# A fused long-convolution and Mish-MLP block on one core: the 660 operations in another total order

## The chip, the cores and the metric

The kernel runs on one core of one Trainium2 chip. The metric is the device time of one execution in microseconds; runs are compared by their medians. The engines are called as in the profile: PE is the matmul array (PEld its weight loads), DVE the vector engine, ACT the scalar engine, POOL the GpSimd engine, SP the sync engine, which here only issues DMAs.

## The reference

All tensors are bf16, the sequence S is 2048, the model width D 640, the inner width F 1728.

```python
h  = x + q_ln * y                       # q_ln = layernorm(x), x = A_q
# kv: 4-tap causal shift convolution of k, times v
kv = (sum over t of k[s-t] * shift_k[:, t]) * v
# y: causal convolution along the sequence with a filter as long as it (FFT of length 2S), plus a skip
y  = irfft(rfft(kv, 2S) * rfft(ssm_k, 2S))[:S] + kv * ssm_D
# the MLP: act(u) = u * tanh(softplus(u)) (Mish)
out = h + act(layernorm(h) @ w1 + b1) @ w2
```

## The kernel before, in words

The convolution is done by matmuls with the tables of a two-stage transform of 128 x 16 points. The channels are held in five chunks of 128 (dc = 0 to 4). The program first builds a list of 660 named operations; each has its engine (or a choice), its dependencies and an emit function (`OP`, class `_Op`). A string `ORDER` then names all 660 in one total order, and `_ordered` emits them in it. An engine works through its own operations strictly in the order of that list, whatever else is ready; between engines only the dependencies count. A token may carry two marks: `@n` places the operation's result in PSUM slot n (there are four slots of 128 x 1024 f32, and a slot is filled again only when its last reader is done), and `:a`, `:d`, `:p` choose ACT, DVE or POOL where the first choice is not meant. DMAs named `d_..`, `sw..` and `tr..` are issued by SP in the order of the list; `d_cst`, `d_sk` and `d_dr` are issued by ACT, and the three small loads of the bias by POOL, within `small`.

The operations by name, in the order of the data:

- `wm` (L292): nine matmuls of zeros that warm PE up; `warm` (L284): loads ACT's function table.
- `d_n0..4`: the filter's five chunks; `dadd0..4` (L370) adds the skip ssm_D to the first tap, with `dsel`, `dcol` (L279, L280) made from `d_dr`; `k1pe0..4` (L376): 16 transposes each, `k1ev` empties them to SBUF.
- `s1kpe dc_g` (L396, L397): the filter's first transform stage, 20 PSUM tiles, emptied by `s1kev`; it needs `d_cst`. `s2kpe_f`, `s2kev_f` (L422): its second stage, in 22 blocks of up to six frequencies, with the table G (`d_g0..7`).
- `b1pe` (L498): transposes the MLP's bias b1, which `small` has loaded (L298, L300); `c_b1` copies it out. `cfpe` (L304): spreads the shift taps (`d_cst`, `d_sk`) over the partitions; `coef` (L309) copies them out, `wsh0..3` (L317) build the shift matrices from them.
- `ktpe`, `ktev` (L341): transposes of k; `kspe dc_h` (L357, L358): the shift convolution, 10 tiles; `kv dc_h` (L362): times v, on DVE.
- `s1vpe`, `s1vev`: the first transform stage of V, the product kv (20 tiles); `s2v0`, `s2v2`, `s2v1`: its second stage, 20 blocks.
- `sw dc_i` (L450): ten DMAs that swap the halves of the filter's spectrum; they need every `s2kev`. `pr dc_f` (L461): 20 products of the two spectra on DVE.
- `i1pe`, `i1ev` (L479): the inverse's first stage, 20 tiles, each needing all four products of its chunk; `i2a`, `i2b`, `i2pe` (L531): its second stage, one per tile of 128 tokens; `y` empties it.
- `ln1_t`, `ln1p t`, `lnx t` (L510 to L524): layernorm of x for token tile t, on DVE, POOL, and ACT or POOL; `wb`, `h` (L538, L540): times y, plus x; `bn`, `pow`, `hc` (L544 to L559): the second layernorm; `trpe`, `trev` (tiles 0 and 1 on PE) or `tr` (a DMA transpose, the others): its result with the channels on partitions.
- `m1pe u_f`, `hb u_f` (L598 to L620): the MLP's first matmul with Mish, in five units of 256, 256, 512, 512 and 512 tokens; `m2pe t` (L663, L671), `res`, `d_out`: its second, the sum with h and the store. `d_w1..` and `d_w2a..c` load the weights.

The casts from PSUM to SBUF of most stages (`ev`, L261 on ACT, L263 on DVE) share one line; they are told apart by their tiles: uv for k's transposes, V and the inverse, ks for the filter and y.

Of the kernel before, what the change touches and what calls it, by code (L numbers as in the profile page):

```python
# [30 lines left out]
ktpe0_3 ktpe0_2 s1kev1_2 ktpe2_0@3 ktpe2_3 ktpe2_2 d_v2 ktpe2_1 ktpe0_1 ktev2 ktpe1_0@1 ktev0:a ktpe1_1 ktpe1_3 ktpe1_2 s1kpe3_3@0 d_g5 ktev1 ktsh2
s1kpe4_0@3 s1kev3_3 s1kpe1_1@2 ktsh0 s1kev4_0:d d_v3 s1kpe4_2@1 wsh0 s1kev1_1 s1kpe3_0@0 s1kev4_2:d s1kpe2_3@3 s1kev3_0 d_g3 ktpe4_0@2 ktpe4_2 ktpe4_3
s1kev2_3 ktsh1 ktpe3_0@1 ktpe4_1 ktpe3_3 ktev4 ktpe3_1 ktpe3_2 s2kpe_6@0 s2kpe_12@3 ktev3 s2kev_6 kspe0_0@2 s2kev_12 s2kpe_18@0 kv0_0 ktsh3 kspe2_0@1
s2kev_18 ktsh4 s2kpe_42@3 kv2_0 kspe3_0@2 s2kev_42 s2kpe_96@0 kv3_0 s2kpe_24@1 s2kev_96 kspe4_0@3 s2kev_24 kspe1_0@2 kv4_0 s2kpe_108@0 kspe1_1@1 kv1_0
# [8 lines left out]
s2v2pe_80@2 pr1_96 s2v2ev_32 s2v2pe_112@1 s2v2pe_64@3 s2v2ev_112 pr1_0 s2v2pe_48@0 s2v2ev_64 s2v2pe_0@1 pr0_96 s2v2ev_0 s2v2pe_16@3 pr1_32 s2v2ev_16
s2v1pe_96@1 pr0_64 s2v2ev_48 i1pe1_1@3 s2v2ev_80 s2v2pe_96@0 pr3_0 s2v1ev_96 i1pe1_2@2 pr3_32 i1ev1_1 s2v1pe_64@1 pr0_32 s2v2ev_96 s2v1pe_0@3 i1ev1_2
pr0_0 s2v1pe_32@0 s2v1ev_0 pr3_64 i1pe1_3@2 d_w14 s2v1ev_64 d_w10 i1pe0_2@3 pr3_96 d_w11 s2v1ev_32 d_w12 i1pe0_1@1 pr4_0 d_w13 i1ev1_3 d_t2m i1pe3_3@0
i1ev0_1 pr2_96 i1pe3_1@2 i1ev3_3 pr2_64 i1pe3_0@1 i1ev0_2 i1pe0_3@0 pr2_0 i1ev3_0 i1pe0_0@3 pr2_32 i1ev3_1 i1pe3_2@1 i1ev0_3 pr4_96 i1pe2_0@2 i1ev0_0
# [687 lines left out]
```

## Time and profile before

| | |
|---|---|
| three runs | 225.21, 226.12 (median), 226.17 us |
| profiled execution: span of its instructions | 223.5 us; its own full time is not on the page |
| busy: PE, PE weight loads | 214.0, 157.6 us |
| busy: DVE, ACT, POOL | 133.2, 133.0, 58.9 us |
| moved by DMA | 30.98 MB, mean 139 GB/s |

The span runs from the first to the last instruction. A matmul is pipelined, so a busy PE need not be at its peak. A row of the timeline reads: start, length, engine, line, operation, output and input tiles, shape, count, and in brackets the idle time before it with what ended it. A row of the groups reads: line, engine, operation, tiles, shape, count, then busy time, mean ns of one, and idle time before.

### The profile page before, as it was taken

What the parts mean: (1) busy time and instruction counts of PE and PEld (TensorE: products, weight loads), DVE (VectorE), ACT (ScalarE), POOL (GpSimd) and SP (SyncE); (2) the same over time, 40 slices, a digit from 0 to 9 for tenths busy, and PEclk for the clock granted to TensorE, in tenths of its full rate; (3) what the DMA queues carried; (4) which work ended last, traced back from release to release, by engine and by line L of the source; (5) the groups of instructions that cost most, each with busy time, mean ns of one, the idle gap of its engine ahead of it and who ended that gap; (6) DMA issues with size and microseconds to landing.
All of it is one profiled execution on the core that took longest, in us unless ns stands there. A gap on an engine that the chain in (4) does not pass through costs nothing.

```text
span 223.5 us, 6119 instructions
## 1 busy us (share of the span) xinstructions
PE 214.0 (96%) x2645; PEld 157.6 (70%) x2650; DVE 133.2 (60%) x232; ACT 133.0 (59%) x182; POOL 58.9 (26%) x120
## 2 busy tenths in 40 slices
PE   7899999999879999889999999999999999999994
PEld 2899999888869999458877644444567444766763
DVE  2776899999989999889878999100002200022122
ACT  2389888999999999999983015565600075200000
POOL 5147620102860005347887523100000000000000
PEclk9999999999999999999999999999999999999999
DMA  5999994372991789303004443500001100010211
GB/s 181 390 413 409 412 374 121 143 239 93 375 415 69 258 331 290 124 0 62 1 0 62 84 123 91 118 0 0 3 0 59 59 3 0 0 56 6 76 54 49
DMA packets 19563, 30.98 MB, mean 139 GB/s; under 512 B 10704, under 2 KB 14928, under 8 KB 18768
## 3 DMA queue, kind: packets, MB, share of 16 engines
q1 hardware_dynamic: 19104, 30.46, 39.0%
q8 instruction: 21, 0.34, 0.7%
q10 hardware_dynamic: 336, 0.12, 0.2%
q14 instruction: 6, 0.05, 0.1%
q0 software_dynamic: 96, 0.00, 0.0%
HBM read 20.42 MB, written 2.62 MB: 103 GB/s over the span
## 4 chain that ended last, share of the span: by engine, by line
PE 70%; DVE 13%; DMA 9%; ACT 4%; issue 2%; SPq 1%; POOL 1%; DVEq 0%
PE ps L663 26%; PE ps L598 25%; DVE ks L461 6%; DMA ks<-in_B_w_dram 4%; DMA ks<-ks 3%; PE ps L396 3%; PE ps L422 3%; ACT uv L261 3%; DMA ks<-in_A_ssm_k_dram 3%; PE ps L341 2%; PE ps L376 2%; DVE ks L263 2%; PE ps L357 2%; DVE ra L362 1%; PE ps L397 1%
## 5 line engine op out<-in xcount | busy, mean ns | idle before, releaser
L620 ACT ACTIVATE ks<-ps,b1s 128x512 bf16<-128x512 f32 (+1 forms) x69 | 36.1, 610 | 42.8 <-PE ps L598 30.3
L663 PE MATMUL ps<-ks 128*128 128x320 bf16 (+2 forms) x420 | 58.4, 299 | 0.0
L598 PE MATMUL ps<-G 128*128 128x512 bf16 (+1 forms) x320 | 57.0, 336 | 0.3
L688 DVE TENSOR_TENSOR rb<-ps,rb 128x640 bf16<-128x640 f32 x15 | 11.7, 816 | 68.9 <-PE ps L671 66.5
L663 PEld LDWEIGHTS <-ks 128*128 128x128 bf16 x420 | 40.6, 98 | 17.2 <-issue 1.3
L598 PEld LDWEIGHTS <-G 128*128 128x128 bf16 x325 | 31.3, 98 | 24.4 <-issue 1.1
L261 ACT CAST uv<-ps 128x1024 bf16<-128x1024 f32 x49 | 45.2, 1197 | 0.0
L261 ACT CAST ks<-ps 128x960 bf16<-128x960 f32 (+3 forms) x49 | 39.8, 905 | 8.1 <-PE ps L397 5.0
L461 DVE TENSOR_TENSOR ks<-ks,uv 128x2048 bf16<-128x2048 bf16 x20 | 23.1, 1225 | 0.7 <-DMA ks<-ks 0.7
L422 PEld LDWEIGHTS <-G 128*128 128x128 bf16 x512 | 20.9, 96 | 3.1 <-issue 2.5
L479 PE MATMUL ps<-a_t,ks 128*128 128x128 bf16 x320 | 18.8, 219 | 0.4 <-DVE ks L461 0.3
L479 PEld LDWEIGHTS <-ks 128*128 128x128 bf16 x320 | 18.3, 113 | 0.7 <-DVE ks L461 0.6
L422 PE MATMUL ps<-uv,G 128*128 128x64 bf16 (+1 forms) x384 | 12.8, 186 | 1.8 <-ACT uv L261 1.8
L544 DVE BATCH_NORM_STATS2 st<-rb 128x6 f32<-128x320 bf16 x32 | 14.0, 478 | 0.1
L515 POOL TENSOR_SCALAR ve<-mv 128x1 f32<-128x1 f32 x16 | 4.7, 292 | 34.9 <-DVE mv L511 34.2
L510 DVE BATCH_NORM_STATS2 st<-rb 128x6 f32<-128x320 bf16 x32 | 13.7, 471 | 0.0
L263 DVE CAST uv<-ps 128x1024 bf16<-128x1024 f32 x11 | 12.9, 1204 | 0.1
L362 DVE TENSOR_TENSOR ra<-ps,rb 128x1024 bf16<-128x1024 f32 x10 | 11.9, 1222 | 0.7 <-PE ps L358 0.5
L524 POOL TENSOR_SCALAR ra<-rb,r,nmr 128x640 bf16<-128x640 bf16 x8 | 8.9, 1118 | 10.0 <-PE ps L397 9.3
L422 PE MATMUL ps<-ks,G 128*128 128x160 bf16 x128 | 11.2, 230 | 0.0
L396 PE MATMUL ps<-cst,ra 128*64 128x128 bf16 x160 | 10.6, 219 | 0.7 <-ACT uv L261 0.5
L263 DVE CAST ks<-ps 128x1024 bf16<-128x1024 f32 (+1 forms) x9 | 10.5, 1197 | 0.5 <-PE ps L422 0.3
(71 smaller groups left out, 256.1 us busy)
## 6 DMA issues: line engine op xcount, KB each, us to landing
ks<-ks SPq DMA_DIRECT2D x10, 512.0 KB, 6.2
G<-tab_g SPq DMA_DIRECT2D x8, 512.0 KB, 11.4
...
```

The source lines that it names most:

```text
L261: nc.scalar.copy(o, i)
L263: nc.vector.tensor_copy(o, i)
L362: nc.vector.tensor_tensor(kv_w[:, m, :, 8 * h:8 * h + 8, :], p_.f32().rearrange("p (l t d) -> p d t l", l=4, t=8), raw_v[:, 8 * h:8 * h + ...
L396: nc.tensor.matmul(ps[0:64, dgl, :], lhs, mc, start=True, stop=True)
L422: nc.tensor.matmul(p_.f32()[:, o:o + n], g_v[:, f, :], src[:, :, f, :], start=True, stop=True)
L461: nc.vector.tensor_tensor(o, o, v, ALU.mult)
L479: nc.tensor.matmul(pz[:, dgl, :], KS[:, k, b, :, l], a12[:, k, :], start=k == 0, stop=k == 1)
L510: nc.vector.bn_stats(st1[:, t, hh, :], xt(t)[:, hh * 320:(hh + 1) * 320])
L544: nc.vector.bn_stats(st2[:, t, hh, :], xt(t)[:, hh * 320:(hh + 1) * 320])
L598: nc.tensor.matmul(ph[:, o:o + w], w1[:, dc, fc * P:fc * P + P], lt[:, dc, 0:w], start=dc == 0, stop=dc == NDC - 1)
L620: nc.scalar.activation(hb[:, fc, 0:n], p_.f32()[:, i * 512:i * 512 + n], ACT.Mish, bias=b1s[:, fc:fc + 1], scale=1.0)
L663: nc.tensor.matmul(p_.f32()[:, o:o + n], lhs, w2[:, k, cols:cols + n], start=fc == 0, stop=single and fc == 13)
```

## The change

Only the string `ORDER` changes: the same 660 names in another total order, with other PSUM slots and, for some, another engine. On ACT's side, `k1ev4`, `ktev0`, `y0`, `y13`, `trev0` and some casts go to DVE and others come from it (`ktev3`, for one); `wsh2` and `wsh3` go from POOL to DVE; `lnx4`, `lnx8`, `lnx9` and `lnx11` go from ACT to POOL and `lnx13` the other way. The first lines of both lists, the stretch in which the filter's second stage meets V's first, and the stretch from the inverse to the MLP:

```diff
 ORDER = """
-d_dr wz idn d_n0 cz wm@0 small lane d_n1 d_cst d_sk d_n2 warm d_n3 d_n4 d_g0 dsel dcol dadd0 d_k2 k1pe0@1 d_k3 dadd1:p k1pe1@2 d_a12 k1ev0b d_k0 k1ev0
-s1kpe0_3@3 k1ev1 s1kpe0_1@0 s1kev0_3 d_k1 s1kpe0_0@1 dadd2 s1kev0_1 s1kpe1_3@2 s1kev0_0:d dadd3:p d_g4 s1kpe0_2@3 k1pe2@0 s1kev0_2 dadd4:p d_g1
-s1kev1_3 kz b1pe@1 k1pe4@3 k1ev2 c_b1 cfpe@2 k1pe3@1 k1ev4:a coef d_v0 s1kpe2_0@0 k1ev3 wsh1 s1kpe2_1@2 s1kev2_0 s1kpe4_3@3 d_g7 s1kev2_1:d s1kpe3_1@1
...
-s2kev_54 s2kpe_60@3 s2kev_84 ln1_0 kspe2_1@1 s2kev_60 s2kpe_48@0 kv2_1 ln1p0 s1vpe0_2@2 s2kev_48 s1vpe1_1@3 s1vev0_2:d s1vpe2_1@1 d_x2 s1vev1_1
...
-s1vpe0_3@1 s1vev1_2 s1vpe1_3@0 s1vev0_3:d s1vpe0_1@2 s1vev1_3 s1vpe3_0@3 s1vev0_1:d s1vpe4_1@1 s1vev3_0 s2kpe_30@0 s1vev4_1:d s2v0pe_0@2 s2kev_30
...
-pr4_32 i1pe1_0@0 i1ev2_0 i1pe2_2@3 pr4_64 i1ev1_0 i1pe2_1@2 ln1_8 i1ev3_2 i1pe2_3@0 i1ev2_2 ln1_6 ln1p8 i1pe4_3@1 i1ev2_3 ln1_11 i1pe4_0@3 ln1p6
...
-trpe1@2 y11 i2pe7@3 hc0 y13 h2 trpe0@1 trev1:a wb3 i2pe6@0 bn2 trev0:a i2pe10@2 y7 m1pe0_3@1 h3 lnx11 pow2 bn3 m1pe0_2@3 y6 hc2 y10 pow3 ln1_7
...
+idn wz small d_n0 warm d_sk lane d_dr d_cst wm@0 cz dsel dcol dadd0 b1pe@1 d_n1 cfpe@2 coef d_n2 d_n3 k1pe0@3 dadd2:p c_b1 d_n4 dadd1 k1pe1@0 k1ev0
+k1ev0b s1kpe0_1@1 k1ev1 dadd3 s1kpe0_0@2 wsh1 d_g0 dadd4:p wsh2:d k1pe2@3 d_k2 s1kev0_1 k1pe3@0 s1kev0_0 d_k3 k1ev2 wsh0 s1kpe1_3@1 k1ev3 s1kev1_3
...
+ktpe4_0@3 ktpe4_3 ktpe4_1 ktpe4_2 kspe1_1@0 s2kpe_120@1 ktev4 s2kpe_0@2 s2kev_120 d_v1 kspe1_0@3 s2kpe_114@1 s2kev_0 kv1_1 ktsh4 ktsh0 kspe3_0@0
...
+s2kpe_66@1 kspe0_1@3 s1vpe1_1@0 s2kpe_42@2 s2kev_66 s1vev1_1 kspe4_0@1 kv0_1 s2kpe_96@3 ktsh2 kv4_0 kspe2_1@0 s2kev_42 s1vpe0_0@2 s2kev_96 kv2_1
...
+s2kev_72:d s2kpe_30@0 s1vpe2_1@1 s1vev1_3:d ln1_1 s2kpe_60@2 s2kev_30 s1vpe3_2@3 d_t2m s1vpe4_3@0 s1vev2_1 s2kev_60 s1vpe3_0@1 s2v0pe_16@2 s1vev3_2:d
+s1vev4_3 d_x1 s1vev3_0:d sw1_1 sw1_0 sw0_1 s2v0pe_96@3 s2v0ev_96:d s2v0pe_112@0 s2v0ev_16 s2v0ev_112 s2v0pe_0@1 s1vpe4_1@2 s2v0pe_80@3 s2v0pe_64@0
...
+pr4_96 i1ev0_2 i1pe2_3@3 ln1_0 ln1_2 i1pe4_1@0 i1pe2_0@2 i1ev2_3 i1ev4_1 ln1_3 i1pe4_3@1 i1ev2_0 i1pe4_0@3 ln1_7 i1pe4_2@0 i1ev4_3 i2a1@2 lnx1:p
+i1ev4_2 i1ev4_0:d i2a3@1 ln1_12 i2a0@3 i2b1 ln1p0 i2b0 y1 i2pe12@0 y0:d i2b3 y12 y3 lnx5:p lnx0:p wb1 ln1p3 i2pe10@2 lnx3:p i2pe8@3 y10 ln1p2 d_w14
...
+w2z trpe0@1 trev0 h3 bn3 pow3 bn2 hc3 d_w12 d_w11 pow2 trev1:a d_w13 hc2 ln1_11 tr3 y11 i2pe9@0 y7 ln1_6 ln1_9 m1pe0_6@1 m1pe0_2@3 m1pe0_4@2 wb5
...
+hb1_1 ln1p15 d_w2c lnx9:p hb1_3 ln1p10 ln1p8 h4 wb9 bn5 pow6 pow5 pow7 bn4 pow4 d_w2b m1pe1_2@3 hc6 hc5 hb1_0 d_w2a h11 i2pe14@2 i2pe13@1 hb1_5 hb1_2
+lnx12 h9 y13:d m2pe0@0 m2pe1@3 lnx15 ln1_14 hc4 hc7 lnx8:p tr5 y14 lnx10 bn9 m2pe2@2 tr6 pow9 wb10 res2 res0 bn11 wb15 lnx13 tr4 wb8 hc9 wb12 tr7
...
 """.split()
```

More of the change, by code (lines that the diff above doesn't have):

```diff
@@ L31 @@
[L31 to L34, printed above, removed]
@@ L43 @@
[L43 to L46, printed above, removed]
@@ L51 @@
-m1pe0_1@0 tr2 lnx8 ln1p10 hc3 hb0_3 m1pe0_5@2 wb8 tr3 hb0_2 h8 ln1p7 m1pe0_6@1 ln1_9 hb0_5 m1pe0_4@3 hb0_1 ln1p14 ln1_15 m1pe0_0@2 hb0_6 lnx4 wb6 w2z
-m1pe1_0@0 wb11 lnx10 wb4 lnx7:p hb0_4 m1pe1_4@1 ln1_5 ln1p15 hb1_0 m1pe1_5@3 wb7 hb0_0 h4 ln1p5 hb1_4 m1pe1_3@0 bn8 hb1_5 lnx5:p m1pe1_1@2 ln1_13
-hb1_3 pow8 m1pe1_2@1 wb5 hb1_1 h6 ln1p9 lnx15 m1pe1_6@3 bn6 hb1_2 h5 i2pe9@0 pow6 hb1_6 bn4 i2pe14@2 lnx9 ln1p13 m2pe0@1 hc6 ln1_12 y9 tr6 y14 lnx13:p
-bn5 lnx14 pow4 hc8 h11 pow5 tr8 m2pe1@3 wb14 h7 ln1p12 hc5 hc4 bn7 tr4 lnx12 wb10 pow7 tr5 bn11 m2pe2@0 h10 pow11 bn10 wb13 pow10 hc7 hc11 tr7 wb9
```

38 lines of the change are left out of this document (23 added, 15 removed).

## The prediction

> **What bounds the kernel now.** I read the windows by stage first, cut where the trace changes hands: the first transpose of the filter at 5.41 us, the last chunk of the filter's second stage at 44, the inverse's first stage from 67 to 89.4, the first FFN matmul at 99.4, the last matmul's end at 220.6.
>
> ```profile
> span 223.5 us, 6119 instructions
> ```
>
> ```profile
> core 0: us, PE busy (x) PEld busy (x) DVE busy (x) ACT busy (x) POOL busy (x), PEclk, DMA share, GB/s
> 0.00:5.40 5.40, 4.02 (x9) 1.19 (x9) 1.10 (x6) 1.49 (x2) 3.09 (x13) 1.00 0.52 173
> 5.40:44.00 38.60, 37.84 (x718) 36.14 (x718) 31.99 (x36) 31.14 (x34) 12.22 (x18) 1.00 0.85 330
> 44.00:67.00 23.00, 20.54 (x597) 18.63 (x595) 21.80 (x26) 23.00 (x26) 10.43 (x16) 1.00 0.70 272
> 67.00:89.40 22.40, 22.05 (x449) 21.62 (x446) 22.30 (x28) 22.40 (x26) 2.97 (x7) 1.00 0.66 237
> 89.40:99.40 10.00, 8.65 (x69) 4.81 (x67) 8.80 (x25) 9.64 (x16) 4.00 (x11) 1.00 0.22 70
> 99.40:220.60 121.20, 120.88 (x819) 75.21 (x822) 46.83 (x115) 45.30 (x82) 26.15 (x57) 1.00 0.16 40
> ```
>
> Three things are to be seen. From 99.4 on PE is busy 120.88 of 121.20 us: what follows the first FFN matmul is a block of fixed length, so the end moves with that matmul's start. From 5.4 to 44 PE leads (37.84 of 38.60), while ACT idles 38.60 - 31.14 = 7.5 us. From 44 to 89.4 ACT is busy 45.40 of 45.40 us: it empties PSUM and sets the pace, with DVE close behind. The instruction span is 223.5 us and the median of the runs 226.12 (225.21 to 226.17); the page has no full time of the profiled execution, so I take 226.12 - 223.5 = 2.6 us as lying around the span, unchanged.
>
> **The change, step 1: the head of PE's queue.** All 660 operations stay, so every difference is order, engine and wait. Before, PE runs the warm-up and then k1pe0. After, b1pe and cfpe stand between. b1pe transposes the bias that POOL's three small DMAs bring, cfpe needs cst and sk_r from ACT's queue, and everything of PE is queued behind them; DVE and ACT have only PE's results to empty.
>
> ```profile
> 1.25 4.02 PE L292 MATMUL ps<-rw 128*128 128x512 bf16 x9 [1.25 <-DVE rw L287]
> 5.41 1.36 PE L376 MATMUL ps<-ident,ks 128*128 128x128 bf16 x16
> 7.20 1.20 PE L376 MATMUL ps<-ident,ks 128*128 128x128 bf16 x16 [0.42 <-DMA ks<-in_A_ssm_k_dram]
> ```
>
> ```profile
> 2.29 0.77 POOL L298 DMA_DIRECT2D b1b<-in_B_b_dram  x1 [0.30 <-POOL b1b L297]
> 3.07 1.01 POOL L300 DMA_DIRECT2D b1b<-in_B_b_dram  x2
> ```
>
> The landings of these three (the answer for tile b1b), ACT's queue at the start, and how long two of its transfers took:
>
> ```profile
> DMA to landing us min/median/max: 5.2/5.3/5.5
> ```
>
> ```profile
> 0.73 0.64 ACTq L271 DMA_DIRECT2D dful<-in_A_ssm_D_dram  x1
> 1.40 0.60 ACTq L269 DMA_DIRECT2D cst<-tab_cst  x1
> 2.03 0.45 ACTq L270 DMA_DIRECT2D sk_r<-in_A_shift_k_dram  x1
> 2.51 1.28 ACT L284 ACT_TABLE_LOAD   x1 [2.51 <-issue]
> 3.81 0.20 ACT L284 ACTIVATE warm<-warm 128x2 f32<-128x2 f32 x1
> ```
>
> ```profile
> cst<-tab_cst ACTq DMA_DIRECT2D x1, 104.0 KB, 4.3
> ...
> sk_r<-in_A_shift_k_dram ACTq DMA_DIRECT2D x1, 5.0 KB, 4.9
> ```
>
> POOL's order is kept, so its third DMA is again issued at 3.07 + 1.01/2 = 3.6 us and lands 5.2 us later, at 8.8. On ACT the table load now goes ahead of the three DMAs; the last of these, cst, is issued at about 0.7 + 1.3 (table) + 0.2 (warm) + 0.45 (sk_r) + 0.65 (dful) = 3.3 us and lands by 3.3 + 4.9 = 8.2. So b1pe runs at 8.8, cfpe at 8.9, k1pe0 at 9.1 instead of 5.41. Before, the front waits for its second block until 7.20 anyway; after, DVE first makes coef (four casts, 1.0 us from 9.3) and dadd1, so k1pe1 starts at 10.5. The front comes 3.3 us later, and ACT's first cast at 12.3 instead of 9.01. Nothing hides it: PE leads here. Between the ends, no wait and 3.7 us, I take 3.3.
>
> A rule speaks against this wait. The Trainium skill, "DMA: Bandwidth & Descriptors", section "Anatomy of one DMA", gives a fixed cost of about 2.0 us for a small DMA of this path; by it the bias would be there at 5.6, the wait would be 0.2 us, and step 1 would cost almost nothing. The row says 5.2 to 5.5 for these very DMAs, beside the same filter loads, and the row decides.
>
> **Step 2: what ACT carries until its last i1 cast.**
>
> ```profile
> 9.01 3.76 ACT L261 CAST ks<-ps 128x1024 bf16<-128x1024 f32 x4 [5.00 <-PE ps L397]
> ...
> 13.44 1.87 ACT L261 COPY ks<-ps 128x2048 bf16<-128x2048 bf16 x1 [0.59 <-PE ps L376]
> 15.30 5.59 ACT L261 CAST ks<-ps 128x1024 bf16<-128x1024 f32 x6
> ...
> 53.42 37.73 ACT L261 CAST uv<-ps 128x1024 bf16<-128x1024 f32 x41
> 91.51 6.66 ACT L261 CAST ks<-ps 128x640 bf16<-128x640 f32 x11 [0.36 <-DMA ks<-in_B_w_dram]
> ```
>
> ```profile
> L261 ACT CAST ks<-ps 128x960 bf16<-128x960 f32 x18 | 16.3, 973 | 2.7 <-PE ps L422 2.5
> ```
>
> One cast of 1024 takes 5.59/6 = 0.93 us (s1k) or 37.73/41 = 0.92 (s1v, s2v, i1), a copy 1.87, an s2k cast 16.3/18 = 0.90. Counted in the two lists: before, ACT has 14 s1k, 2 copies, 19 s2k and 49 of V and i1, that is 13.0 + 3.7 + 17.1 + 45.1 = 78.9 us; after, 15, 1, 18 and 48, that is 14.0 + 1.9 + 16.2 + 44.2 = 76.3. ACT loses 2.6 us of work, to DVE. Before, 9.0 + 78.9 leaves 3.3 us idle until its last i1 cast ends at 91.2. After, I followed the four PSUM slots by hand down the new list: ACT waits 1.3 us behind k1pe3, 1.2 where the last s1k casts meet the first s2k block, and some 1.0 in pieces, 3.5 in all. So 12.3 + 76.3 + 3.5 = 92.1, 0.9 us later than before. Of the 3.3 us lost at the head, 2.4 come back.
>
> **Step 3: V's first stage among the filter's second.** It fills PSUM slots while the products kv are made, and leaves filter blocks for later: by hand the last of them (s2kev_60) is emptied at 54.8, where the first swap was issued at 53.6.
>
> ```profile
> 53.63 11.52 SPq L450 DMA_DIRECT2D ks<-ks  x10
> ```
>
> ```profile
> 65.28 19.39 DVE L461 TENSOR_TENSOR ks<-ks,uv 128x2048 bf16<-128x2048 bf16 x17 [0.69 <-DMA ks<-ks]
> ```
>
> ```profile
> L263 DVE CAST uv<-ps 128x1024 bf16<-128x1024 f32 x11 | 12.9, 1204 | 0.1
> ...
> L317 POOL TENSOR_TENSOR rw<-cst,coef 128x1120 bf16<-128x1120 bf16 x4 | 8.2, 2063 | 2.8 <-DVE coef L309 2.8
> ...
> L540 DVE TENSOR_TENSOR rb<-ks,rb 128x640 bf16<-128x640 bf16 x16 | 7.5, 473 | 0.1
> ```
>
> ```profile
> ra<-tab_t2m SPq DMA_DIRECT2D x1, 1024.0 KB, 9.1
> ```
>
> The 1.2 us are covered: DVE has V casts until 61.0, and the ten swaps, issued each 1.15 us, stay ahead of their products (pair 0 wanted at 65.7, landed about 65). d_t2m and d_x1 now stand in SP's queue before the swaps, the first with 1.0 MB; at the 330 GB/s of the second window's row that is 3 us, begun at 51.5, when V's stage has read what it overwrites. It is over by the first swap, and I cost it at 0, with 2 us if the swaps are held up. DVE then has 20 products, one ln1 and one cast: 61.0 + 20 x 1.14 + 1.0 + 1.1 = 85.9 (1.14 is 19.39/17). The last product frees the last five i1 blocks, 5 x 0.9 on PE, so the last cast ends about 91.8: the same as ACT's own sum. wsh2 and wsh3 move from POOL to DVE, which no row shows: between 0.73 us (640 columns at 0.47, the rest at the products' rate) and POOL's 2.06. I take 1.2, what a DVE pass over 1024 columns costs, since one operand is broadcast along its last axis; they fall where PE leads, so the ends give -0.3 to +1.
>
> **Step 4: from the last i1 cast to the first FFN matmul.** y1 starts at 92.4 (91.51 before). y0 goes to DVE and delays wb1 by 0.2; the chain wb, h, bn, hc, trpe, trev has the same members. The first FFN matmul then comes at 100.3, where it was 99.4: +0.9. Two of the sixteen i2 blocks are left for later in both lists, so PE's remaining block is equal.
>
> **Step 5: the FFN.** w2 is now issued behind tr3 and tr2, at about 107, and lands about 116; m2pe0 wants it at 117. POOL takes three more lnx (11 instead of 8), so the last transposed tile of the third unit lands near 131.7, wanted near 132.
>
> ```profile
> ks<-in_B_w_dram SPq DMA_DIRECT2D x1, 2080.0 KB, 8.7
> ```
>
> ```profile
> L516 POOL TENSOR_TENSOR r<-ve,mhalf 128x1 f32<-128x1 f32 x16 | 9.5, 593 | 1.3
> L524 POOL TENSOR_SCALAR ra<-rb,r,nmr 128x640 bf16<-128x640 bf16 x8 | 8.9, 1118 | 10.0 <-PE ps L397 9.3 <-POOL nmr L517 0.2
> ```
>
> From 105 POOL has nine ln1p (about 1.3 each: 0.59 and two small ones), five lnx (1.0) and four pow (1.0): 21 us, to 126; then hc4, hc7 and two transposes. I cost both at 0; if a cover fails it is a wait of up to 2 us.
>
> **Step 6: the array after the pause.** The warm-up matmul of 512 columns takes 4.02/9 = 0.45 us; in the FFN the same width goes in half that:
>
> ```profile
> 134.63 12.04 PE L598 MATMUL ps<-G 128*128 128x512 bf16 x54
> ```
>
> (12.04/54 = 0.22.) So the array starts at half rate and had risen by 7.20 (1.20/16 = 0.075 for a transpose of 128 columns), although the page's clock row reads 1.00 there. Before, the pause between warm-up and k1pe0 is 0.1 us; after, it is 5.3 to 8.8, 3.5 us. No row shows such a pause with work behind it. If the array falls back, the 32 transposes of k1pe0 and k1pe1 and a few s1k blocks go at half rate: 32 x 0.06 = 1.9 us at most, part of it beside DVE's coef; nothing if it does not fall. I take 1.1. The Trainium skill, "TensorE: Matmul & The Clock Gate", section "Part 1: The HAM clock gate", says that after one idle window of about 3.4 us the array goes at half its rate until a busy window has passed; by that rule this pause is just long enough, and which way it falls is chance.
>
> **The sum.** Head +3.3, ACT's lighter load -2.4, the way to the FFN 0.0, half rate +1.1: +2.0. A span of 225.5, a time of 225.5 + 2.6 = 228.1 us.
>
> **The rivals.** (a) *The array stays at full rate*: the same without +1.1, 227.0. For it: the warm-up is only just over. (b) *A cover fails in the FFN*, w2 or POOL's chain, whose margins are 1 us and 0.3: +1 to +2 more, 229 to 230.5. For it: hand-followed times leave out small latencies; against it: PE has had such margins before and waited 0.3 us in 121. (c) *Faster*: the bias lands before k1pe0's data. Then the head costs at most 0.3, ACT's 2.6 us come through, the first FFN matmul is at about 97.5 and the time 224.2. It decides at a landing by 5.4 us, so at 1.8 us after issue; the rows say 5.2. (This is what the rule of step 1 comes to.) The same time comes if ACT's idle 3.5 us of step 2 vanish. (d) *No effect*: the head is lost and wholly won back, 226.1; PE's 0.76 us of idleness from 5.4 to 44 speaks against it, ACT's 7.5 for it.
>
> **How the numbers follow.** Forecast 0.38, (a) 0.24, (b) 0.13, (c) 0.15, (d) 0.10. Half a per cent is 1.1 us, about what a measurement of this kernel can tell from no change; the bounds are 225.0 and 227.25. Slower: most of the forecast (0.32), a third of (a), all of (b): 0.53. Faster: (c) and little else: 0.16. The rest, 0.31, is within. The range must leave out no more than 0.2: from 224.6, inside (c), where some of its gain is kept, to 230.6, the end of (b).
>
> **What would show it.** In the trace after: b1pe at 8.8 and k1pe0 at 9.1 (step 1); the 16 transposes of k1pe0 in 1.2 or 1.9 us (step 6); ACT's first cast at 12.3 to 13.5 and its last i1 cast at 92 to 93.5 (step 2); the first swap near 55 and products without waits from 61 (step 3); the first FFN matmul at 100.3 to 101.5 and 121 us from there to the last one (steps 4 and 5). Wrong would be a k1pe0 before 6 us, an FFN start before 99, or PE waiting by more than 1 us after it.

## The result and the profile after

| | before | after |
|---|---|---|
| runs, us | 225.21, 225.61, 226.12, 226.17 | 235.39, 235.64, 236.04, 236.32 |
| median | 225.87 | 235.84 |
| span of the profiled execution | 223.5 | 234.3, in a run of 236.04 |

The ratio is 1.0452, with an interval of 1.0426 to 1.0479: slower by 4.5%, where 228.1 us were forecast and the range ended at 230.6. About 1.8 us lie around the span (236.04 - 234.3), not 2.6.

The windows of the kernel after, with the bounds at its own handovers: PE's first wait ends, the last transpose of k ends, the first swap is issued, the last i1 cast ends, the first FFN matmul starts, the last matmul ends. After each stretch stand its length, the busy times of PE, PEld, DVE, ACT and POOL, the granted clock of PE, and what the DMAs did.

```profile
0.00:9.63 9.63, 3.78 (x10) 1.22 (x11) 1.34 (x7) 1.49 (x2) 3.39 (x14) 0.92 0.76 275
9.63:33.90 24.27, 24.18 (x442) 22.04 (x443) 19.69 (x22) 16.23 (x17) 5.70 (x10) 0.89 0.98 396
33.90:60.50 26.60, 26.34 (x531) 24.00 (x531) 24.09 (x23) 23.54 (x28) 2.42 (x5) 1.00 0.19 57
60.50:99.40 38.90, 34.55 (x790) 32.60 (x790) 36.73 (x45) 36.86 (x40) 9.76 (x15) 1.00 0.67 253
99.40:107.20 7.80, 7.46 (x62) 4.34 (x60) 7.34 (x20) 7.41 (x14) 6.09 (x12) 1.00 0.00 0
107.20:229.40 122.20, 121.40 (x824) 75.06 (x821) 51.46 (x125) 42.67 (x78) 30.67 (x66) 1.00 0.21 52
```

The last window ends 0.2 us too early: the last matmul ends at 227.91 + 1.70 = 229.6, and the table below goes by that.

```profile
227.91 1.70 PE L663 MATMUL ps<-ks 128*128 128x256 bf16 x14
```

The same handovers in the kernel before (its FFN is the last row of the prediction's windows, 121.20):

```profile
0.00:5.41 5.41, 4.02 (x9) 1.19 (x10) 1.10 (x6) 1.49 (x2) 3.09 (x13) 1.00 0.52 173
5.41:27.40 21.99, 21.34 (x442) 20.09 (x443) 16.09 (x20) 16.82 (x17) 10.95 (x15) 1.00 1.02 406
27.40:53.60 26.20, 25.90 (x548) 24.58 (x548) 25.09 (x25) 23.92 (x28) 2.22 (x5) 1.00 0.55 196
53.60:91.20 37.60, 34.22 (x772) 32.13 (x772) 36.63 (x51) 37.55 (x41) 13.82 (x25) 1.00 0.77 289
91.20:99.40 8.20, 7.62 (x61) 4.41 (x61) 7.07 (x19) 7.89 (x14) 2.63 (x6) 1.00 0.03 6
```

The table to keep in mind is the difference of the lengths. The last column is the experiment a11_all, told of below, between its own handovers.

| stage | before | after | difference | three repairs |
|---|---|---|---|---|
| to the end of PE's first wait | 5.41 | 9.63 | +4.2 | 5.2 |
| filter's first stage, k's transposes | 21.99 | 24.27 | +2.3 | 24.2 |
| V among the filter's second stage, to the first swap | 26.20 | 26.60 | +0.4 | 26.6 |
| swaps, products, to the last i1 cast | 37.60 | 38.90 | +1.3 | 37.9 |
| to the first FFN matmul | 8.20 | 7.80 | -0.4 | 7.7 |
| FFN | 121.2 | 122.4 | +1.2 | 122.8 |
| behind the last matmul | 2.9 | 4.7 | +1.8 | 3.0 |

So the stretch in which the new order puts V among the filter's second stage costs 0.4 us. The loss lies ahead of it and behind it, first of all at the head. The head of PE's queue after, then its waits, then ACT's queue and the first cast, and the landing of the bias (min, median, max):

```profile
9.63 0.17 PE L498 MATMUL ps<-ident,b1b 14*128 14x14 bf16 x1 [4.61 <-DMA b1b<-in_B_b_dram]
9.65 0.22 PE L304 MATMUL ps<-sk_r,cst 32*128 32x80 bf16 x1
9.81 3.63 PE L376 MATMUL ps<-ident,ks 128*128 128x128 bf16 x32
```

```profile
PE ps L498 <- DMA b1b<-in_B_b_dram: 4.6, 1, 4.6
...
PE ps L422 <- issue: 0.9, 1, 0.9
PE ps L479 <- issue: 0.9, 1, 0.9
```

```profile
0.72 1.28 ACT L284 ACT_TABLE_LOAD   x1 [0.72 <-PEq L718]
...
2.33 0.64 ACTq L269 DMA_DIRECT2D cst<-tab_cst  x1
9.83 0.17 ACT L499 CAST b1s<-ps 128x14 f32<-128x14 bf16 x1 [7.61 <-PE ps L498]
14.48 1.93 ACT L261 CAST ks<-ps 128x1024 bf16<-128x1024 f32 x2 [4.47 <-PE ps L397]
```

```profile
DMA to landing us min/median/max: 5.6/5.9/6.2
```

PE stands idle for 4.61 us until the bias lands, 5.9 us after the last of its DMAs was issued (at 3.6), and then does 32 transposes in 3.63 us (1.36 + 1.20 = 2.56 before). ACT's first cast comes at 14.48, 5.5 us after the 9.01 of before. From 9.63 to 14.48 the granted clock is 0.50. In the page's clock row this dip is seen too, and the gap in PE's row ahead of it:

```profile
PE   6399999999958989999999999999999999999992
...
PEclk9679999999999999999999999999999999999999
```

The clock row doesn't show every such dip. In a1_bias, told of next, the same 32 transposes took 3.64 us after a wait of 4.38, and its clock row reads 9 in every slice; the duration of the matmuls is the surer sign.

### The profile page after: what moved, and what is told of

Same layout as the page of the kernel before. It is cut to its first block, busy times and chain, and to the rows that moved or that the text cites. A ratio compares the mean times of both kernels' runs of the same rounds, so it can differ in the third digit from the quotient of the medians.

```text
span 234.3 us, 6110 instructions
## 1 busy us (share of the span) xinstructions
PE 217.9 (93%) x2650; PEld 159.3 (68%) x2650; DVE 141.3 (60%) x240; ACT 128.2 (55%) x174; POOL 58.0 (25%) x120
## 4 chain that ended last, share of the span: by engine, by line
PE 69%; DVE 11%; ACT 9%; POOL 4%; issue 3%; DMA 3%; POOLq 0%
PE ps L663 19%; PE ps L598 18%; PE ps L479 7%; PE ps L422 6%; PE ps L396 6%; ACT uv L261 5%; PE ps L376 3%; ACT ks L261 3%; DVE st L510 3%; PE ps L341 3%; DMA b1b<-in_B_b_dram 3%; DVE st L544 2%; PE ps L357 2%; PE ps L358 1%; DVE ks L538 1%
## 5 line engine op out<-in xcount | busy, mean ns | idle before, releaser
L620 ACT ACTIVATE ks<-ps,b1s 128x512 bf16<-128x512 f32 (+1 forms) x69 | 36.6, 594 | 48.1 <-PE ps L598 40.5
L598 PE MATMUL ps<-G 128*128 128x512 bf16 (+1 forms) x325 | 57.8, 337 | 0.8 <-DMA G<-rw 0.4
L261 ACT CAST ks<-ps 128x960 bf16<-128x960 f32 (+3 forms) x47 | 39.3, 901 | 9.6 <-PE ps L397 6.9
L422 PEld LDWEIGHTS <-G 128*128 128x128 bf16 x512 | 20.6, 96 | 5.0 <-issue 3.6
L479 PE MATMUL ps<-a_t,ks 128*128 128x128 bf16 x320 | 18.7, 219 | 1.4 <-issue 0.9
L479 PEld LDWEIGHTS <-ks 128*128 128x128 bf16 x320 | 18.2, 114 | 1.7 <-issue 1.1
L685 DVE TENSOR_TENSOR rb<-ps,rb 128x384 bf16<-128x384 f32 (+1 forms) x2 | 1.0, 491 | 27.1 <-PE ps L663 27.1
L515 POOL TENSOR_SCALAR ve<-mv 128x1 f32<-128x1 f32 x16 | 3.8, 235 | 53.6 <-DVE mv L511 52.9
L422 PE MATMUL ps<-uv,G 128*128 128x64 bf16 (+1 forms) x384 | 12.8, 187 | 3.2 <-ACT uv L261 2.0
L263 DVE CAST uv<-ps 128x1024 bf16<-128x1024 f32 x12 | 14.3, 1216 | 1.7 <-PE ps L422 0.9
L263 DVE CAST ks<-ps 128x1024 bf16<-128x1024 f32 (+2 forms) x11 | 12.0, 1122 | 1.0 <-PE ps L397 0.4
L524 POOL TENSOR_SCALAR ra<-rb,r,nmr 128x640 bf16<-128x640 bf16 x11 | 12.3, 1124 | 0.2
L397 PE MATMUL ps<-cst,ks 128*64 128x128 bf16 x160 | 11.8, 229 | 0.0
```

What stands on the lines that cost most here:

```text
L261: nc.scalar.copy(o, i)
L263: nc.vector.tensor_copy(o, i)
L422: nc.tensor.matmul(p_.f32()[:, o:o + n], g_v[:, f, :], src[:, :, f, :], start=True, stop=True)
L479: nc.tensor.matmul(pz[:, dgl, :], KS[:, k, b, :, l], a12[:, k, :], start=k == 0, stop=k == 1)
L524: nc.gpsimd.tensor_scalar(lnx_s[t % 9], xt(t), r1[:, t:t + 1], nmr1[:, t:t + 1], ALU.mult, ALU.add)
L598: nc.tensor.matmul(ph[:, o:o + w], w1[:, dc, fc * P:fc * P + P], lt[:, dc, 0:w], start=dc == 0, stop=dc == NDC - 1)
```

## The experiments

The theory was made of three parts: **T1**, the head (bias wait and half rate) makes a loss of about 5.5 us that nothing swallows; **T3**, the loads beside the swaps and the new order cost a few us in the middle; **T2**, the order of the stores on SP costs 1.8 us at the end. The rival to T1 was that slack downstream swallows the head's loss. All ratios are against the kernel before (225.2 to 225.8 us on these chips). The changed kernel has 1.0426 to 1.0479.

### The head, undone and transplanted

**a1_bias**, only b1pe and c_b1 later:

```diff
-... dadd0 b1pe@1 d_n1 cfpe@2 coef ... dadd2:p c_b1 d_n4 ... k1pe4@3 s1kpe0_2@1
+... dadd0 d_n1 cfpe@2 coef ... dadd2:p d_n4 ... k1pe4@3 b1pe@1 c_b1 s1kpe0_2@1
```

> One part undone: only b1pe and c_b1 go back behind k1pe4, cfpe and the rest of the head stay as changed. Theory T1 (what stands ahead of the filter in PE's queue costs its wait, and the loss is carried to the end): k1pe0 is then held by cst and the taps alone (cst landed at 8.5 us, b1b at 9.6), so k1pe0 starts about 0.9 us earlier, at about 8.9, and the time is about 0.9 us below the changed kernel's 235.8: 234.9. Rival (slack downstream swallows what the head loses): k1pe0 moves as said, the time stays within 0.4 us of 235.8.

Measured 236.17 us, ratio 1.0479 (1.0448 to 1.051): nothing gained. Of its waits and of its issues to landing:

```profile
PE ps L304 <- DMA cst<-tab_cst: 4.4, 1, 4.4
```

```profile
cst<-tab_cst ACTq DMA_DIRECT2D x1, 104.0 KB, 7.3
```

cfpe now held PE until cst landed, 2.33 + 7.3 = 9.6 us, and k1pe0 stayed at 9.8. Two gates stood there, one behind the other: in this execution ACT's late load cost as much as POOL's bias, so taking the bias away alone was worth nothing. The expectation failed by taking cst's landing from the trace of the changed kernel, where it came at 2.33 + 6.2 = 8.5. Why the same DMA, issued at the same 2.33, took 7.3 us here is not shown.

**a3_warm**, `WARM = 9` to 26, the array kept busy through the wait:

> The changed kernel with 26 warm-up matmuls for 9, so that the array is busy until b1b lands and no pause of 4.6 us comes before k1pe0. If the half rate after the pause is a loss (step 6 of the prediction): k1pe0's 16 transposes in 1.2 us or less in place of 1.7, and a time about 1 us below the changed kernel, 234.8. Rival: what DVE and ACT do beside hides it, 235.8 within 0.4.

```profile
1.25 7.62 PE L292 MATMUL ps<-rw 128*128 128x512 bf16 x26 [1.25 <-DVE warm L283]
...
9.82 2.22 PE L376 MATMUL ps<-ident,ks 128*128 128x128 bf16 x32
```

Measured 235.28, ratio 1.0441 (1.0419 to 1.0463). The 32 transposes take 2.22 us for 3.63 and ACT's first cast comes at 12.65 for 14.48, so the half rate after the pause is real and is 1.8 us at that place. At the end about 0.6 is seen (1.0 was expected), which the intervals do not separate from 0: at k1pe4 PE then waited 1.56 us for a slot that DVE emptied late, a wait that the half rate had covered. DVE was held up by wsh2, which ran beside POOL's wsh0:

```profile
13.67 2.89 DVE L317 TENSOR_TENSOR rw<-cst,coef 128x1120 bf16<-128x1120 bf16 x1
...
24.83 1.32 DVE L317 TENSOR_TENSOR rw<-cst,coef 128x1120 bf16<-128x1120 bf16 x1
```

```profile
13.32 2.07 POOL L317 TENSOR_TENSOR rw<-cst,coef 128x1120 bf16<-128x1120 bf16 x1
```

Alone (wsh3 at 24.83) the operation takes DVE 1.32 us, beside POOL's 2.89. In the changed kernel wsh2 overlaps POOL's wsh0 for 0.6 us instead of 1.7 and takes 1.81.

**a2_head**, the whole head undone, and **a6_head_dve** and **a9_head_pool**, the same with DVE relieved. The diff is that of a9_head_pool, in which wsh3 too goes from DVE to POOL. a6_head_dve has k1ev4:a besides; a2_head leaves wsh2 and wsh3 on DVE and has cfpe@2 coef wsh1 wsh2:d behind k1ev4 and wsh0 behind s1kpe4_3:

```diff
-idn wz small d_n0 warm d_sk lane d_dr d_cst wm@0 ... dadd0 b1pe@1 d_n1 cfpe@2 coef d_n2
+d_dr d_cst d_sk idn wz small d_n0 warm lane wm@0 ... dadd0 d_n1 d_n2
-k1pe4@3 s1kpe0_2@1 s1kev0_3 s1kev0_2 s1kpe1_1@0 k1ev4 s1kpe3_3@2
+k1pe4@3 cfpe@0 coef b1pe@1 c_b1 s1kpe0_2@1 s1kev0_3 s1kev0_2 s1kpe1_1@0 k1ev4 wsh1 wsh2 wsh0 wsh3 s1kpe3_3@2
```

> The whole head undone, the rest of the changed order left: d_dr, d_cst and d_sk lead ACT's queue ahead of its table load, b1pe and c_b1 stand behind k1pe4, cfpe, coef and the three first wsh behind the filter's first blocks. T1: k1pe0 at about 5.5 us, the first ACT cast at about 9, all of the following stages some 4 to 5.5 us earlier, the time about 5 us below the changed kernel: 230.5 to 231.5. Rival (absorbed): k1pe0 at 5.5 as well, but the first FFN matmul by no more than 2 us earlier than 107.2, the time above 233.8. What then remains above the kernel before (about 5 us) belongs to other parts of the list.

> The head undone again, and this time DVE relieved as before: wsh2 and wsh3 on POOL, k1ev4 on ACT, cfpe and coef right behind k1pe4 in a slot that DVE empties at once. In the kernel with only the head undone, PE got 4.2 us at k1pe0 but the last transpose of k came only 3.0 us earlier: two blocks of the filter's first stage waited 1.1 us each, for coef and for DVE's casts behind coef and wsh2. Theory T1b (head and DVE's added work together are the filter stage's loss): the last transpose of k ends at 28.5 to 29.5, the time is 5.5 us below the changed kernel, 230.3. Rival (loads bound the stage until 34 us, the head's wait is mostly cover for them): not below 232.8.

> The head undone, wsh2 and wsh3 on POOL, cfpe and coef behind k1pe4 in slot 0; k1ev4 stays on DVE, since in the kernel that gave it to ACT a filter block waited 1.7 us for its slot. Theory T1b (a stage with no slot held is PE's work alone): the last transpose of k ends at 29 to 30 (35.4 in the changed kernel) and the time is 231 to 232. Rival (what is left of the 5.2 us is in the order of the filter's own blocks): no better than 233.3, as the two earlier kernels with the head undone.

| | k1pe0 | last transpose of k evacuated | time | ratio |
|---|---|---|---|---|
| after | 9.8 | 35.4 | 235.84 | 1.0452 |
| a2_head | 5.6 | 32.4 | 233.32 | 1.035 (1.0333 to 1.0367) |
| a6_head_dve | 5.2 | 32.5 | 233.37 | 1.034 (1.0284 to 1.0396) |
| a9_head_pool | 5.3 | 31.0 | 232.28 | 1.0276 (1.0213 to 1.034) |

PE's waits between 5 and 36 us, in a2_head and then in a6_head_dve:

```profile
PE ps L396 <- DVE coef L309: 1.1, 1, 1.1
PE ps L396 <- DVE ks L263: 1.1, 1, 1.1
```

```profile
PE ps L396 <- ACT ks L261: 1.7, 1, 1.7
```

Each waited for an evacuation that I had put badly: for coef and DVE's casts behind it in a2_head, for k1ev4 on ACT in a6_head_dve, where the rival's number (not below 232.8) held but not its reason. a2_head's 233.3 lies between the 231.5 of T1 and the 233.8 of its rival, and settles neither. With both mended, a9_head_pool gives back 4.4 us at the last transpose of k and 3.5 in the median of the whole time (4.0 by the ratios). Its four executions run from 230.72 to 232.93, and the profiled one, the fastest, is 5.5 us shorter than the profile of the changed kernel. So head and wsh together are worth 3.5 to 4 us here in the middle of the executions, less than the 5.5 of T1.

**b1_head_after**, the changed head on the list of before:

```diff
-d_dr wz idn d_n0 cz wm@0 small lane d_n1 d_cst d_sk d_n2 warm ... dadd0 d_k2 k1pe0@1 ... kz b1pe@1 k1pe4@3 k1ev2 c_b1 cfpe@2 k1pe3@1 k1ev4:a coef
+wz idn d_n0 warm d_sk d_dr d_cst cz wm@0 small lane d_n1 d_n2 ... dadd0 b1pe@0 cfpe@2 coef d_k2 k1pe0@1 c_b1 ... kz k1pe4@3 k1ev2 k1pe3@1 k1ev4:a
```

> The list of before with the changed head alone: table load first on ACT, then d_sk, d_dr, d_cst; b1pe, cfpe and coef ahead of k1pe0. If the head's wait is carried to the end whatever follows (T1): k1pe0 at 9.5 us, the first ACT cast 4.5 to 5.5 us later than 9.0, the time 4 to 5.5 us above before, 229.5 to 231. Rival (in either list about half of it is cover for the filter's loads and for DVE's work, as the 2.5 us from undoing it suggest): 2 to 3 us above, 227.4 to 228.4.

Measured 231.09, ratio 1.0245 (1.0189 to 1.0301). b1pe waits 5.1 us for the bias, k1pe0 starts at 10.6, and the 5.2 us are still there at y1 (96.7 for 91.5) and at the last matmul. In an order with PE full, the head's whole loss is carried; the rival falls there. In the changed order less comes back when the head is undone. The waits of 1.1 and 1.7 us above are such as the head's loss had covered; that nothing else makes the difference is not shown.

### Splitting the lists

**c1_filter_before** (before up to the last transposes of k, then the changed list), **c2_filter_after** (the reverse), **b3_ffn_before** (changed up to i1ev4_0, then before), **b2_ffn_after** (before up to i1ev4_1, then changed). What the second list still has to name follows in its order. **c1b_filter_before** is c1_filter_before with the loads in the changed list's order:

```diff
-d_g4 d_g1 d_v0 d_g7 d_v1 d_g2 d_g6 d_v2 d_g5 d_v3 d_g3
+d_g6 d_v2 d_v3 d_g7 d_v0 d_v1 d_g5 d_g2 d_g4 d_g1 d_g3
```

> The list of before up to the last transposes of k (its head, its filter's first stage), from there the changed list: V among the filter's second stage, the changed FFN and the changed tail. The changed kernel is 10.4 us above the kernel before; its last transpose of k ends 7.2 us later (35.4 against 28.2). T1 (head and filter's first stage lose what the end shows): this kernel is 10.4 - 7.2 = 3 us above before, 228.5. Rival T3 (V among the filter's second stage and the transfers beside it are the greater part): 5 us or more above before, over 230.5. Second rival (the moved V gains by itself): at most the tail's 1.8 above before, under 227.2.

> The complement: the changed list up to the last transposes of k, from there the list of before. T1: 6.5 to 7.2 us above the kernel before, 232 to 232.6. T3: less than 5 us above it, under 230.4. If the two parts do not act on each other, this difference and that of the kernel with before's filter sum to 10.4.

> The changed list up to the inverse's first stage (i1ev4_0), then the list of before: FFN and stores in their old order. The changed kernel lost 8.2 us at its last i1 cast and 10.8 at its end, so the FFN with the tail is worth 2.6: 233.2 expected. Rival (POOL's chain or w2 in the changed order was no cost, and the rest is the clock): within 0.5 of 235.8.

> As the earlier kernel with before's filter and the changed rest, with one thing mended: that kernel's product kv1_1 waited 5.0 us for d_v3, which before's list issues late; here the loads after d_k1 go in the changed list's order (d_g6, d_v2, d_v3 first). T1 (the changed list from the last transposes of k on loses only in FFN and tail): 3 us above the kernel before, 228.5. T3 (V among the filter's second stage and the transfers beside the swaps cost by themselves): 4.5 us or more above, over 229.8. Second rival (the moved V gains): under 227.2.

> The list of before up to the inverse's first stage (i1ev4_1), then the changed list: FFN and stores alone in their new order. The changed kernel lost 8.2 us up to the last i1 cast and 10.8 at the end: by this 2.6 us above the kernel before, 228.0, of which 1.8 behind the last matmul and about 1 within the FFN. Rival (step 5 of the prediction, FFN at nothing): only the tail, at most 1.8 above, 227.2 or less.

| | time | ratio |
|---|---|---|
| c2_filter_after | 233.69 | 1.0366 (1.035 to 1.0381) |
| c1_filter_before | 236.35 | 1.0491 (1.0472 to 1.051) |
| c1b_filter_before | 230.59 | 1.0226 (1.0186 to 1.0266) |
| b2_ffn_after | 227.15 | 1.0071 (1.0046 to 1.0095) |
| b3_ffn_before | 241.04 | 1.0705 (1.0663 to 1.0748) |

c2_filter_after bears T1 out, with more than the 6.5 to 7.2 expected: 8.4 us, carried whole from the last transpose of k (+7.5) to the end. Two of the five told more of their joints than of their parts. The 236.35 of c1_filter_before would speak for T3 (over 230.5), but its first product waits for a load of v (`d_v3`), which before's list issues late. The 241.04 of b3_ffn_before missed both of its expectations: the layernorm steps that before has among V fall together on POOL at the joint, and hc, which PE waits for, is late:

```profile
DVE ra L362 <- DMA rb<-in_A_v_dram: 5.0, 1, 5.0
```

```profile
PE ps L569 <- DVE rw L559: 4.4, 1, 4.4
```

The other two give shares: b2_ffn_after +1.7 for FFN and stores, c1b_filter_before 5.2, which leaves 3.4 for the middle. These shares are not absolute: 8.4 for head and filter's first stage (c2_filter_after) and 5.2 for all the rest make 13.6, where the whole change costs 10.0, so the parts act on each other. The middle's 3.4 is above the +1.7 of the windows. In c1b_filter_before's own profile the stretch to the first swap is 1.5 us longer than before (0.4 in the changed kernel), since ACT waits 3.2 us for its s2k block at the joint, 1.4 in the changed kernel; the stretch from there to the last i1 cast is 1.2 longer (1.3 in the changed kernel). The excess is the joint again, so the 5.2, which meet T3's 4.5, hold about 1.1 of it.

b2_ffn_after came out at the number of its rival (1.8 at most, the stores alone), but not by the rival's reason: in its profile the FFN is 122.5 us long (+1.3) and 3.9 us lie behind the last matmul (+1.0). Its FFN shows one wait:

```profile
PE ps L598 <- ACT ks L620: 1.0, 1, 1.0
```

The changed kernel's own FFN has others: 0.4 us for a transposed tile (at 114.9) and 0.3 ahead of the third unit, where the kernel before has none.

### The loads among the swaps

**b4_t2m** on the changed kernel, **c4_t2m** on c1b_filter_before:

```diff
-s1vpe3_2@3 d_t2m s1vpe4_3@0 ... s1vev4_3 d_x1 s1vev3_0:d sw1_1 sw1_0 ... sw4_1 d_w10
+s1vpe3_2@3 s1vpe4_3@0 ... s1vev4_3 s1vev3_0:d sw1_1 sw1_0 ... sw4_1 d_t2m d_x1 d_w10
```

> The changed kernel with d_t2m (1.0 MB) and d_x1 behind the ten swaps on SP's queue, nothing else moved. T3's part (these two loads lie in the rings beside the swaps, the swaps land 6.4 to 7.8 us after issue, and PE's instructions come late: gaps of 0.9, 1.6 and 0.9 us that nothing else explains): the swaps land in 4 to 6 us, the gaps at 65, 68 and 82 us go or halve, the time 1 to 3 us below 235.8. Rival (the gaps come from the order of PE's instructions or from the swaps alone; step 3 costed these loads at nothing): 235.8 within 0.5.

> The kernel with before's filter stage and the changed rest (230.6) with d_t2m and d_x1 behind the swaps. If their place is a third or more of the middle's 3.4 us: 229.4 or less, and the two stretches in which PE waits for nothing but its own instructions (0.9 us each) go or shrink. Rival: the middle's loss is ACT's and DVE's order, these loads are 0.8 us as in the changed kernel or less: 229.8 to 230.6.

Measured 235.02 (1.0428, 1.0404 to 1.0451) and 229.03 (1.0138, 1.0087 to 1.019): 0.8 us and 1.6 us less than their parents. Each gain taken alone is at the edge of the noise (the intervals overlap those of the parents), and 0.8 is less than the 1 to 3 expected; the traces are clearer. The matmuls of one V block (s2v0pe_48) in the changed kernel, then in b4_t2m:

```profile
64.82 0.37 PE L422 MATMUL ps<-uv,G 128*128 128x64 bf16 x7
66.12 0.34 PE L422 MATMUL ps<-uv,G 128*128 128x64 bf16 x6 [0.93 <-issue]
```

```profile
63.81 0.87 PE L422 MATMUL ps<-uv,G 128*128 128x64 bf16 x24
```

The gap of 0.93 us, for which the profile names no other engine and no DMA ("issue"), is gone; the later one at L479 only shrinks (0.9 to 0.7), and in c4_t2m it stays at 1.0. The median swap lands 6.3 us after its issue where it took 7.2.

All profiles together settle it. From the first swap's issue to the end of the last i1 cast (ACT's last cast of 1024 columns), in us, with the sum of PE's gaps of this kind at L422:

| | profiles | first swap to last i1 cast | gaps at L422 |
|---|---|---|---|
| new order of the middle, d_t2m and d_x1 ahead of the swaps | 11 | 38.4 to 40.0 | 0.3 to 1.4 in each |
| the same order, the two loads behind them (b4_t2m, c4_t2m, a11_all) | 3 | 37.6 to 38.0 | none |
| the middle of the list of before | 5 | 37.5 in each | none |

So the place of the two loads makes 1.0 us and more of the +1.3 of this stretch, and the order of the operations 0.1 to 0.5. T3's part holds in place and sign, below its size. The same gaps vary from one execution to the next, and this is part of the noise in all runs that keep the loads there.

### The stores

**a4_tail** puts every d_out right behind its res; **a5_tail_late** only those from d_out5 on:

```diff
-res15a m2pe14@2 res13 res14 d_out13 ... res8 res15b d_out15a d_out7 d_out6 d_out9 d_out10 d_out8 d_out15b
+res15a d_out15a m2pe14@2 res13 d_out13 res14 d_out14 ... res8 d_out8 res15b d_out15b
```

> The changed kernel with each d_out right behind its res in the list, nothing else moved. T2 (the order of the stores on SP makes the end): after the last matmul the span ends about 1.6 to 1.8 us sooner, 234.1. Rival (the last store lands as late in any order, because the last sum itself is late): 235.8 within 0.4.

> The changed kernel with only the stores from d_out5 on moved, each behind its res; the early ones (d_out2, d_out3, d_out1, d_out0, d_out4) stay where they are, since in the kernel with all stores moved d_out2 and d_out0 stood ahead of the transposes tr4 and tr7 on SP's queue and held them. T2: 1.7 us below the changed kernel, 234.1 (in that kernel the stretch from the last matmul's end to the last store's issue had already gone from 2.8 to 1.1 us). Rival: within 0.4 of 235.8.

a4_tail: 239.75, ratio 1.0634 (1.0592 to 1.0676), 3.9 us slower than the changed kernel. SP's queue near 135 us in a4_tail, and in the changed kernel:

```profile
132.61 2.53 SPq L573 DMA_TRANSPOSE G<-rw  x2
137.98 1.07 SPq L692 DMA_DIRECT2D out_dram<-rb  x2
139.10 2.52 SPq L573 DMA_TRANSPOSE G<-rw  x2
```

```profile
132.55 9.57 SPq L573 DMA_TRANSPOSE G<-rw  x5
```

tr4 and tr7, which the FFN's next matmuls read, stand behind two stores that wait for their sums; tr4 goes at 139.1 instead of 135.4, and PE's third unit starts at 143.1 instead of 139.5, after a pause:

```profile
143.13 0.59 PE L598 MATMUL ps<-G 128*128 128x512 bf16 x1 [3.86 <-DMA G<-rw]
```

The pause costs more than its length: from 143.1 to 150 the granted clock is 0.56, and the unit's first run of matmuls takes 8.4 us for 5.5. The store ready first is not the one to issue first on a shared queue. At the end T2 holds even here: 3.0 us lie behind the last matmul (239.0 - 236.0), 4.7 in the changed kernel. a5_tail_late leaves the early ones alone: ratio 1.0396 (1.0357 to 1.0435), 234.87 us in the median, so about 1 us below the changed kernel for 1.7 expected; the intervals overlap. SP's last stores after, then in a5_tail_late:

```profile
213.45 18.60 SPq L692 DMA_DIRECT2D out_dram<-rb  x12
```

```profile
204.82 24.57 SPq L692 DMA_DIRECT2D out_dram<-rb  x9
```

The issues end 2.4 us behind the last matmul in the one (232.05 against 229.61) and 0.8 in the other (229.39 against 228.57), as in the kernel before (221.36 against 220.55). Behind the last matmul the span has 4.7 us in the one and 3.0 in the other, 2.9 before: the trace shows T2's 1.7 to 1.8 us whole.

### The alternation of two kinds of work on PE

With head and DVE mended, PE's filter stage was still 2 us longer than before's. **d1_switch** puts four blocks of it among k's transposes in the list of before:

```diff
-ktpe0_3 ktpe0_2 ... ktpe1_1 ktpe1_3 ktpe1_2 s1kpe3_3@0 ... s1kpe4_0@3 ... ktpe4_0@2 ktpe4_2 ktpe4_3
+ktpe0_3 s1kpe1_2@0 ktpe0_2 ... ktpe1_1 s1kpe3_3@0 ktpe1_3 s1kpe4_0@3 ktpe1_2 ... ktpe4_0@2 ktpe4_2 s1kpe2_3@3 ktpe4_3
```

> The list of before with four blocks of the filter's first stage (s1kpe1_2, s1kpe3_3, s1kpe4_0, s1kpe2_3) moved in among k's transposes, so that PE alternates between the two four times more often; all else as before. If each alternation costs 0.2 us going and 0.12 us coming back: PE's first stage is 4 x 0.33 = 1.3 us longer (the last transpose of k at 28.7 for 27.4), and the time up to 1.3 us above the kernel before, since PE leads in that stage. Rival (the longer steps in the changed kernel come from waits that the profile does not name, not from the alternation): the steps there keep 0.24 and 0.45 us and the time stays within 0.4 us of before.

Measured 227.53, ratio 1.0101 (1.0083 to 1.0119): +2.35, where at most 1.3 was expected. The 40 transposes of k in before, in d1_switch, and three of the six runs of them in the changed kernel (rows of other lines between are left out):

```profile
19.21 3.14 PE L341 MATMUL ps<-ident,ra 128*128 128x128 f32 x24
...
25.43 2.18 PE L341 MATMUL ps<-ident,ra 128*128 128x128 f32 x16
```

```profile
19.25 0.71 PE L341 MATMUL ps<-ident,ra 128*128 128x128 f32 x4 [0.60 <-DMA ra<-in_A_k_dram]
...
20.46 2.18 PE L341 MATMUL ps<-ident,ra 128*128 128x128 f32 x16
...
23.14 0.50 PE L341 MATMUL ps<-ident,ra 128*128 128x128 f32 x2
...
24.14 0.50 PE L341 MATMUL ps<-ident,ra 128*128 128x128 f32 x2
...
27.05 0.74 PE L341 MATMUL ps<-ident,ra 128*128 128x128 f32 x4
...
28.29 1.70 PE L341 MATMUL ps<-ident,ra 128*128 128x128 f32 x12
```

```profile
24.95 1.22 PE L341 MATMUL ps<-ident,ra 128*128 128x128 f32 x8
...
26.96 1.70 PE L341 MATMUL ps<-ident,ra 128*128 128x128 f32 x12
...
31.89 0.50 PE L341 MATMUL ps<-ident,ra 128*128 128x128 f32 x2
```

A run of n transposes takes 0.12 n + 0.26 us: 24 take 3.14, 2 take 0.50. Six runs instead of two cost about 0.8 us, from start to start, and the way back some 0.1 each. That part of the theory holds with the same figures in the three kernels shown. The other 1.4 us of d1_switch are two waits that the moved blocks ran into, 0.6 for a load of k and 0.8 for a slot that DVE held; 2.35 less 1.4 leaves about 1 us for the alternation.

### The repairs together

**a11_all** is a9_head_pool with the loads of b4_t2m and the stores of a5_tail_late:

> The changed kernel with three repairs together: head and wsh as in a9_head_pool (about -4.2), d_t2m and d_x1 behind the swaps (-0.8), late stores in order (-1.0 measured, -1.7 at best). If they add up: 229.8. If the swaps then only wait where they waited before (they do not add): 231 or more. Still slower than the kernel before in either case, by the middle's and the FFN's own loss.

Measured 229.19, ratio 1.015 (1.0105 to 1.0195): 6.6 us below the changed kernel. They add up (3.5 + 0.8 + 1.0 = 5.3 and somewhat more). Its stages stand in the last column of the first table. What is left is the filter's first stage, 24.2 for 21.99, and the FFN, 122.8 for 121.2. In the filter's first stage PE is busy for 22.66 us (21.34 before), which is about what four more alternations make (0.8 + 4 x 0.1), and idle for 0.9 more. No version here beats the kernel before, and nothing in the runs points to one.

## Why the prediction was wrong

The sign was right, the size was not: +2.0 forecast on the span, +10.8 measured. By its own steps, in us:

| step | forecast | measured |
|---|---|---|
| 1 and 6, up to ACT's first cast | +4.4 | +5.5 |
| 2 and 3, from there to the last i1 cast | -2.4 | +2.7 |
| 4, to the first FFN matmul | 0.0 | -0.4 |
| 5, FFN | 0 | +1.2 |
| behind the last matmul | not named | +1.8 |

**Step 2 failed, and with it the sum.** Its loads were right: ACT's work from its first cast on was put at 76.3 us, and the windows give 76.5 (16.23 + 23.54 + 36.86, less 0.17 for the bias). For the kernel before the 78.9 was a little high (16.82 + 23.92 + 37.55 = 78.3), so ACT was relieved of 1.8 us, not 2.6. Its idle time was put wrongly: 3.5 us by hand against 8.4 (99.4 - 14.48 - 76.5). The windows of before had said that PE leads from 5.4 to 44; step 1 used it, and step 2 did not: it let ACT win back idle time in a stretch that PE sets, and "followed the four PSUM slots by hand" with blocks of constant length. PE was busy 24.18 of 24.27 us up to the last transpose of k, and its blocks had grown, by the half rate at first and by four more alternations. A lighter ACT wins nothing where PE feeds it. Of the 8.4 us of idle time, 3.4 lie before the last transpose of k and 3.1 from there to the first swap, in both of which PE is full (50.5 of 50.9 us). The other 2.0 lie behind the first swap, where ACT was idle for 0.05 us before; they fall to 1.0 in a11_all, where the two loads of step 3 stand behind the swaps. "Of the 3.3 us lost at the head, 2.4 come back" had this as its only ground, and b1_head_after shows the opposite.

**Step 1** was right in its mechanism, a little small: the bias landed 5.9 us after issue (5.2 taken) and k1pe0 came at 9.8 (9.1). The trace is far from the Trainium skill's 2.0 us for such a DMA ("DMA: Bandwidth & Descriptors", "Anatomy of one DMA"), as the prediction had argued. That cst came at 8.5, near the 8.2 reckoned, was luck: ACT's queue began to issue at 1.25, during the table load (0.72 to 2.00), so that cst went at 2.33 and not at 3.3, and it took 6.2 us to land and not 4.9. What the step missed is that cst is a second gate at about the same time (a1_bias).

**Step 6** was right: the array fell to half rate in the pause and a3_warm shows it by taking the pause away. Its size was 1.8 us at ACT's first cast (1.1 taken). The Trainium skill's rule of one idle window of about 3.4 us ("TensorE: Matmul & The Clock Gate", "Part 1: The HAM clock gate") agrees with a pause of 4.61.

**Step 3**: the stage itself was right, +0.4. Costing d_t2m and d_x1 at nothing was wrong; they are worth 0.8 to 1.6 (b4_t2m, c4_t2m), inside the 2 us named as the other end. d_t2m went at 57.17 and not at 51.5, and landed at 62.0, behind the first swap's issue at 60.50 and not before it. One sum of the step is off by 0.5 us (85.9 + 5 x 0.9 and a last cast of 0.9 make 91.3, not 91.8); nothing hung on it, since ACT's own sum came later, at 92.1. wsh on DVE took 1.8 and 1.3 us for 1.2 each, more where POOL ran one at the same time.

**Step 4** was right. **Step 5**: w2 was in time, and the cover of the transposed tiles failed by 0.4 and 0.3 us. The FFN cost 1.2 all the same; b2_ffn_after, with the same FFN, had its 1.0 us of waiting at a Mish result, which no step had named. What makes the rest is not shown.

**The stores** are in no step. The same d_out names stand in another order at the end of the list, and the prediction took "what follows the first FFN matmul" as a block of fixed length up to the end. That holds to the last matmul and not behind it.

**The rivals**: (c) and (d) rested on the same idle ACT and fall with it; (b) was the nearest. The range was too narrow because it priced each edit's own bounds and not the one assumption beneath step 2.

Open: what is late in PE's gaps of 0.9 us. That those at L422 go with the place of the two loads was shown, though both loads had landed (57.17 + 4.8 and 57.53 + 6.8) when the gap began at 65.2; the one at L479 stays in every kernel with the new order of the middle (0.3 to 1.7 us), the loads moved or not. Open too is why the head gives back 5.5 us in one profile and 3.5 to 4 in the middle of the executions.
